# P v with [v|ones] as one full-width stationary operand, q and k loaded in 8-token runs, and layer 1 of the first chunk issued ahead of batch 1's attention

## The chip, the cores and the metric

The kernel runs on one core of one Trainium2 chip. The metric is the device time of one execution in microseconds (us), as the median of several runs. Each run carries a state, fast or slow (a slower state that some executions fall into whatever the kernel); unless a slow run is named, all times, ratios and profiles here are of fast runs. A ratio is the mean time of one kernel's fast runs over the mean of the other's fast runs of the same rounds, on the same chip, so it is not quite the ratio of the medians quoted beside it. The runs were made on several chips, so the cost of a step between two kernels is taken from the difference of their ratios, times 362.4 us. Intervals are 95%.

In the profile PE is TensorE (matmuls and transposes), PEld its weight loads, DVE is VectorE, ACT is ScalarE, POOL is GpSimd. PEclk is the TensorE clock that was granted, as a share of full speed. SBUF is the on-chip memory that the engines work on, PSUM the one that matmuls write to.

## The reference

```python
# q, k, v: [8 batches, 8 heads, 576 tokens, 64], fp32; w_in: [512, 2048]; w_out: [2048, 512]
rel = pos[:, None] - pos[None, :]
mask_local   = (rel >= 0) & (rel < 32)                       # heads 0 to 3
mask_strided = (rel >= 0) & (pos[None] % 32 == pos[:, None] % 32)   # heads 4 to 7
scores = where(mask, (q @ k.T) / 8, -1e9)
attn = softmax(scores)                                       # over the keys
x = concat_heads(attn @ v)                                   # [4608 tokens, 512]
h = x @ w_in
g = where(h > 0, h, exp(min(h, 0)) - 1)                      # ELU
out = g @ w_out                                              # [4608, 512], fp32
```

## The kernel before

The 4608 tokens are nine chunks of 512. A step of layer 1 (`l1`) is four dense matmuls into `hps`, an exp on ScalarE and two VectorE operations that make one block of `g`. A step of layer 2 (`l2`) is four dense matmuls into `ops`. The attention of a batch is cut into 12 pieces: four T (transposes of q and k for a pair of heads) and eight S (scores, exp, mask). Each S leaves an O (P v and the division) to be done one piece later. Pieces are laid between the dense steps, so that TensorE stays busy while ScalarE and VectorE do the softmax.

```python
    p_wk = ctx.enter_context(tc.tile_pool(name="work", bufs=3))
    p_s = ...  # PSUM, 1 buffer of two banks: scores
    p_a = ...  # PSUM, 3 buffers: tp (transposes), o_ps, s_ps
    p_h = ...  # PSUM, 2 buffers: hps
    p_o = ...  # PSUM, 1 buffer: ops
    # [...]
    def piece_T(P):
        for nm, dst in (("q", P.qT[:, 0:S]), ("k", P.kT[:, PRE:PRE + S])):
            ps = p_a.tile([128, S], BF16, tag="a", name="tp")
            # [...] 8 transposes (6 for k of the local heads) into ps
            nc.vector.tensor_copy(dst, ps)
    # [...]
    def piece_O(P, u, pm):
        o_ps = p_a.tile([128, W], F32, tag="a", name="o_ps")
        s_ps = p_a.tile([128, W], F32, tag="a", name="s_ps")
        # local heads:
        for x in range(2):
            nc.tensor.matmul(s_ps[x * D:(x + 1) * D, :], lhsT=ones, rhs=pm[:, x], ...)
        for i in range(3):
            for x in range(2):
                nc.tensor.matmul(
                    o_ps[x * D:(x + 1) * D, i * LQ:(i + 1) * LQ],
                    lhsT=batch_in[P.b]["vl"][:, (P.g0 + x) * LB + 3 * u + i, :],
                    rhs=pm[:, x, i * LQ:(i + 1) * LQ], ...)
        # [...] strided heads: the same with eight matmuls of 72 columns
        nc.scalar.activation(ln, s_ps, ACT.Ln)
        nc.scalar.activation(rc, ln, ACT.Exp, scale=-1.0)      # 1 / sum
        # [...]
        nc.vector.tensor_mul(dst, o_ps..., rc...)              # into xT
    # [...]
    def run_piece(p, lag=0, split=False):
        kind, P, u = p
        flush(lag)                                # O of the older pieces
        if kind == "T":
            piece_T(P)
        else:
            pend.append((P, u, piece_S(P, u, split)))
    # [...] batch 0 alone, then:
    for nb in range(NCH):
        for m in range(MC):
            if nb > 0:
                l2(nb - 1, m)
            if done < len(pieces):
                run_piece(pieces[done], lag=1 if nb == 0 else 0)
                done += 1
            else:
                flush()
            l1(nb, m)
            # [...] load the next batch
```

`s_ps` is read by Ln alone, and only `o_ps` waits for the multiply at the end of the division.

The softmax here doesn't subtract the row's maximum and nothing guards it: scores larger than these inputs give would overflow.

## Time and profile before

| | before |
|---|---|
| time, median of 3 runs | 362.39 us (361.56 to 363.46) |
| TensorE busy | 329.1 us, 91% of the span |
| VectorE, ScalarE busy | 243.8 us, 194.3 us |
| share of TensorE in the chain that ended last | 73% |
| granted clock in the profiled stages from 80 us on | 1.00 |

The first lines are from the page of the kernel before: busy time, the timeline in 40 slices (a digit is the busy share in tenths), and the shares of the engines in the chain of waits that ended last.

```profile
PE 329.1 (91%) x2656; PEld 161.5 (45%) x2656; DVE 243.8 (68%) x501; ACT 194.3 (54%) x377; POOL 92.3 (26%) x120
...
PE   1851986999999999999999999999999999999995
...
PEclk9999999899999999999999999999999999999999
...
PE 73%; DMA 12%; ACT 6%; POOL 4%; issue 2%; DVE 2%; ACTq 0%
```

TensorE is saturated from the eighth slice on (63 us), at full clock from the ninth (72 us), and the chain is mostly its own work. The stage table of the kernel before, for one stretch (columns: stretch, its length, busy time and instructions by engine, granted clock, DMA share, GB/s):

```profile
100.00:125.00 25.00, 24.87 (x237) 12.32 (x235) 20.16 (x42) 16.74 (x34) 8.81 (x11) 1.00 0.81 93
```

TensorE works 24.87 of 25 us. The timeline of the kernel before around one O piece (start, duration, engine, line, operation, output from inputs, count, idle time before and what ended it):

```profile
132.88 0.31 PE L270 MATMUL s_ps<-pm,ones 72*64 72x288 bf16 x2
...
133.03 0.30 PE L279 MATMUL o_ps<-pm,vs 72*64 72x72 bf16 x8
...
133.24 0.41 ACT L297 ACTIVATE ln<-s_ps 128x288 f32<-128x288 f32 x1 [0.52 <-PE s_ps L270]
...
133.26 0.43 PE L211 MATMUL tp<-identity,ql 72*128 72x72 bf16 x8
...
133.68 0.44 ACT L299 ACTIVATE rc<-ln 128x288 f32<-128x288 f32 x1
133.70 0.42 PE L211 MATMUL tp<-identity,kl 96*128 96x96 bf16 x6
...
134.16 0.46 DVE L304 TENSOR_TENSOR xT<-o_ps,rc 128x288 bf16<-128x288 f32 x1 [0.25 <-ACT rc L299]
```

The O piece ends at 133.3 us. The q transposes follow at once, and the k transposes at 133.70, as soon as Ln (133.24 to 133.65) has freed the buffer of `s_ps`. The multiply, at 134.16, holds up nobody.

### The profile page before, as it was taken

The numbers are of one execution on the slowest core, as the hardware profiler recorded it, in microseconds if no ns is written. First come the engines' busy times: TensorE is split into PE (matmuls) and PEld (weight loads), VectorE is DVE, ScalarE is ACT, GpSimd is POOL, SyncE is SP. The second block draws the span as 40 slices with busy tenths as digits, with TensorE's granted clock in tenths as the row PEclk, the third lists the DMA queues.
The fourth block names the chain that finished last, engine by engine and source line by source line (L and its number), as shares of the span: only waits on it lengthen the run. The fifth ranks groups of instructions, "written<-read, shape, count | busy, mean of one in ns | idle before, by whom it ended". The sixth has DMA issues, their size and how long they took to land.

```text
span 361.1 us, 6843 instructions
## 1 busy us (share of the span) xinstructions
PE 329.1 (91%) x2656; PEld 161.5 (45%) x2656; DVE 243.8 (68%) x501; ACT 194.3 (54%) x377; POOL 92.3 (26%) x120
## 2 busy tenths in 40 slices
PE   1851986999999999999999999999999999999995
PEld 1630443454544544445454454444444444444442
DVE  2640797787877877777878777776666666666610
ACT  1650575667566666666666666664444433543411
POOL 7952843958507214510620000000000000000000
PEclk9999999899999999999999999999999999999999
DMA  6999999999959965992960111010111110021122
GB/s 91 113 178 178 107 199 158 99 159 152 142 93 102 96 101 72 87 114 63 119 48 29 31 31 31 29 32 29 46 44 30 34 55 29 29 59 31 30 71 76
DMA packets 88321, 29.03 MB, mean 80 GB/s; under 512 B 72672, under 2 KB 83680, under 8 KB 88288
## 3 DMA queue, kind: packets, MB, share of 16 engines
q0 software_dynamic: 82432, 19.14, 61.7%
q1 hardware_dynamic: 5856, 9.44, 9.1%
q8 instruction: 21, 0.34, 0.4%
q14 instruction: 12, 0.10, 0.1%
HBM read 38.21 MB, written 9.44 MB: 132 GB/s over the span
## 4 chain that ended last, share of the span: by engine, by line
PE 73%; DMA 12%; ACT 6%; POOL 4%; issue 2%; DVE 2%; ACTq 0%
PE ops L382 32%; PE hps L347 30%; DMA vs<-in_v_dram 5%; DMA ks<-in_k_dram 5%; PE tp L211 3%; PE tp L203 2%; PE sc L243 2%; ACT e L251 2%; ACT osb L387 2%; DMA vl<-in_v_dram 2%; DVE pm L259 2%; PE s_ps L286 1%; ACT ln L297 1%; PE s_ps L270 1%; POOL kl L85 1%
## 5 line engine op out<-in xcount | busy, mean ns | idle before, releaser
L347 PE MATMUL hps<-xT,w_in_sb 128*128 128x512 bf16 x576 | 151.4, 386 | 0.2
L382 PE MATMUL ops<-w_out_sb,g 128*128 128x512 bf16 x576 | 145.4, 379 | 0.0
L352 ACT ACTIVATE he<-hps 128x512 f32<-128x512 f32 x144 | 85.8, 596 | 103.7 <-PE hps L347 103.0
L382 PEld LDWEIGHTS <-g 128*128 128x128 bf16 x576 | 56.4, 98 | 68.0
L347 PEld LDWEIGHTS <-w_in_sb 128*128 128x128 bf16 x576 | 50.8, 99 | 53.3 <-issue 2.1
L251 ACT ACTIVATE e<-sc 72x576 bf16<-72x576 f32 (+1 forms) x60 | 38.3, 639 | 17.4 <-PE sc L243 17.4
L297 ACT ACTIVATE ln<-s_ps 128x288 f32<-128x288 f32 x64 | 26.3, 411 | 16.9 <-PE s_ps L270 8.7
L387 ACT COPY osb<-ops 128x512 f32<-128x512 f32 x36 | 21.1, 586 | 20.0 <-PE ops L382 20.0
L76 POOL DMA_DIRECT2D ql<-in_q_dram x32 | 27.2, 855 | 18.0 <-PE tp L211 6.6
L299 ACT ACTIVATE rc<-ln 128x288 f32<-128x288 f32 x64 | 28.4, 443 | 2.0
L85 POOL DMA_DIRECT2D kl<-in_k_dram x32 | 23.7, 758 | 19.7 <-DMA ks<-in_k_dram 5.5
L203 PE MATMUL tp<-identity,qs 72*128 72x72 bf16 x128 | 7.9, 213 | 18.4 <-DMA qs<-in_q_dram 18.4
L304 DVE TENSOR_TENSOR xT<-o_ps,rc 128x288 bf16<-128x288 f32 x32 | 14.6, 456 | 8.3 <-ACT rc L299 7.9
L309 DVE TENSOR_TENSOR xT<-o_ps,rc 128x288 bf16<-128x288 f32 x32 | 14.6, 457 | 7.8 <-ACT rc L299 5.0
L253 DVE TENSOR_TENSOR pm<-e,mask_s 72x576 bf16<-72x576 bf16 x32 | 14.5, 452 | 3.8 <-ACT e L251 2.4
L259 DVE TENSOR_TENSOR pm<-e,mask_l 128x576 bf16<-128x576 bf16 x32 | 14.6, 457 | 2.5 <-ACT e L251 0.5
L203 PEld LDWEIGHTS <-qs 72*128 72x128 bf16 x128 | 5.8, 108 | 19.9 <-DMA qs<-in_q_dram 18.7
L67 POOL DMA_DIRECT2D vs<-in_v_dram x8 | 5.7, 710 | 31.9 <-PE sc L243 31.6
L96 POOL DMA_DIRECT2D vl<-in_v_dram x8 | 9.6, 1197 | 11.8 <-PE tp L203 11.4
L286 PE MATMUL s_ps<-pm,ones 128*64 128x288 bf16 x64 | 10.6, 322 | 1.6 <-DVE pm L259 0.9
L203 PE MATMUL tp<-identity,ks 72*128 72x72 bf16 x128 | 7.9, 214 | 3.9 <-DMA ks<-in_k_dram 3.6
L291 PE MATMUL o_ps<-pm,vl 128*64 128x96 bf16 x192 | 10.6, 215 | 0.7 <-DMA vl<-in_v_dram 0.7
(343 smaller groups left out, 338.5 us busy)
## 6 DMA issues: line engine op xcount, KB each, us to landing
out_dram<-osb SPq DMA_DIRECT2D x32, 144.0 KB
qs<-in_q_dram POOLq DMA_DIRECT2D x8, 288.0 KB, 5.9
ks<-in_k_dram POOLq DMA_DIRECT2D x8, 288.0 KB, 7.7
vs<-in_v_dram POOLq DMA_DIRECT2D x8, 288.0 KB, 7.9
ql<-in_q_dram POOLq DMA_DIRECT2D x32, 72.0 KB, 6.3
kl<-in_k_dram POOLq DMA_DIRECT2D x32, 72.0 KB, 4.2
vl<-in_v_dram POOLq DMA_DIRECT2D x8, 288.0 KB, 5.5
w_in_sb<-in_moe_w_in_dram POOLq DMA_DIRECT2D x4, 512.0 KB, 10.9
```

The lines of the kernel that those rows point to most:

```text
L76: nc.gpsimd.dma_start(out=t[:, h // 2, :, h % 2, :], in_=q[b, h].rearrange("(p s) d -> p s d", s=NS))
L85: nc.gpsimd.dma_start(out=t[:, h // 2, :, h % 2, :], in_=src[b, h].rearrange("(t p) d -> p t d", p=LQ))
L203: nc.tensor.transpose(ps[:, o:o + RS], src[:, P.g0 + x, 2 * sp * D:2 * (sp + 1) * D], identity[0:RS, 0:RS])
L251: nc.scalar.activation(e[0:R], sc[0:R, :, 0:W], ACT.Exp, scale=scale)
L259: nc.vector.tensor_mul(pm, e, mb.unsqueeze(1).to_broadcast([128, 2, W]))
L297: nc.scalar.activation(ln, s_ps, ACT.Ln)
L299: nc.scalar.activation(rc, ln, ACT.Exp, scale=-1.0)
L304: nc.vector.tensor_mul(dst, o_ps.rearrange(pat, z=2, sp=2), rc.rearrange(pat, z=2, sp=2))
L347: nc.tensor.matmul(hps, lhsT=w_in_sb[:, cc, m * 128:(m + 1) * 128], rhs=xT[:, cc, nb * CHUNK:(nb + 1) * CHUNK], start=(c == 0), stop=(c == ...
L352: nc.scalar.activation(e, hps, ACT.Exp)
L382: nc.tensor.matmul(ops, lhsT=g[:, m, kk * 128:(kk + 1) * 128], rhs=w_out_sb[:, m, :], start=(m == 0), stop=(m == MC - 1))
L387: nc.scalar.copy(o_sb, ops)
```

## The change

The intent has three parts.

- **P v (P).** The separate ones matmuls go. The stationary operand (the one that is loaded as weights, PEld, before the other streams through) becomes [v|ones] for the first head of a pair and [ones|v] for the second, 128 columns wide, so that one matmul gives both P v and the sums. The two heads then need one PSUM tile each. Two Ln of 64 partitions and two multiplies of 64 partitions replace one each of 128, and both PSUM tiles live until the multiply. For the strided heads VectorE first spreads the loaded v into that layout (`vs`).
- **Loads (L).** q and k of the local heads come in runs of 8 tokens, as one transfer each instead of four. The local heads must be paired on the chip (GpSimd copies `qlp`, `klp`), and the k transposes come out in another order of tokens, which the copy out of PSUM undoes.
- **Order (S).** All of layer 1 of chunk 0 is issued before batch 1's attention, which then runs without dense steps beside it. Later pieces are spread over a chunk's 16 steps, 1.2 steps apart.

```diff
+    def spread_v(b):                       # two VectorE copies per batch
+        t = vss[b % 2]
+        src = batch_in[b]["vr"].rearrange("p (g x) (s d) -> p x g s d", x=2, d=D)
+        for x in range(2):
+            nc.vector.tensor_copy(t[:, :, :, 2 * x * D:(2 * x + 1) * D], src[:, x])
+    def pair_up(b, nm):                    # four GpSimd copies per batch from batch 2 on
+        [...]
+            nc.gpsimd.tensor_copy(t[:, :, :, x, :], src[:, x])
 [... loads ...]
 # piece_T, local heads
+                if nm == "k":
+                    dst = dst.rearrange("c (p s) -> c s p", s=NS)
+                    ps = ps.rearrange("c (s p) -> c s p", s=NS)
             nc.vector.tensor_copy(dst, ps)
 [...]
 # piece_O
-        o_ps = p_a.tile([128, W], F32, tag="a", name="o_ps")
-        s_ps = p_a.tile([128, W], F32, tag="a", name="s_ps")
+        o_ps = [p_a.tile([128, W], F32, tag="a", name=f"o_ps{x}") for x in range(2)]
 [... the ones matmuls go; local heads, strided alike: ]
+            for x in range(2):
+                for i in range(3):
                     nc.tensor.matmul(
-                        o_ps[x * D:(x + 1) * D, i * LQ:(i + 1) * LQ],
-                        lhsT=batch_in[P.b]["vl"][:, (P.g0 + x) * LB + 3 * u + i, :],
+                        o_ps[x][:, i * LQ:(i + 1) * LQ],
+                        lhsT=vt[:, P.g0 // 2, 3 * u + i, x * D:(x + 2) * D],
-        nc.scalar.activation(ln, s_ps, ACT.Ln)
+        nc.scalar.activation(ln[lo], o_ps[0][hi], ACT.Ln)
+        nc.scalar.activation(ln[hi], o_ps[1][lo], ACT.Ln)
         nc.scalar.activation(rc, ln, ACT.Exp, scale=-1.0)
-            nc.vector.tensor_mul(dst, o_ps..., rc...)
+        for x, pr in ((0, lo), (1, hi)):
+            [...] nc.vector.tensor_mul(xs[pr, ...], o_ps[x][pr], rc[pr])
 [... main loop ...]
+    for m in range(MC):
+        l1(0, m)
+    for i in range(PB, 2 * PB):
+        run_piece(pieces[i], lag=1, split=(pieces[i][0] == "S" and pieces[i][2] == 1))
+    flush()
+    for nb in range(1, NCH):
+        [... sorted list of l2 steps, pieces and l1 steps ...]
+            at = [8 + 0.7 * i if nb == 1 else 0.1 + 1.2 * i for i in range(PB)]
```

## The prediction

> **What bounds it now.** From about 62 us on TensorE is the limit: in the table by stages it is busy 24.87 of 25 us at 100 to 125 us. Dense 512-column matmuls follow each other every 0.216 us (timeline: four in 0.86 us), so 1152 of them are 249 us. Until 62 us the timeline shows loads and latency: TensorE waits 9.4 us for batch 1's q, then VectorE and ScalarE set the pace while chunk 0's first layer is mixed with batch 1's attention. Later a step (4+4 dense) takes 1.73 us alone, about 2.49 us with an attention piece: a batch of 12 pieces costs TensorE about 9.1 us.
>
> **Removed.** The ones matmuls: s_ps plus o_ps take 0.37 us per piece; eight (or six) full-width ones should take 0.24. That is about 1 us a batch, 6 to 7 us in all. The small runs of q and k go; v should land about 2.6 us earlier (20.3 before) and w_in by 28 us. The 8.7 us of idle before batch 1 goes.
>
> **Added, with measured durations.** A second Ln per piece (0.41 us ScalarE), a second xT multiply (0.457 us VectorE), two VectorE copies of v a batch (estimate 0.4 to 0.7 us each), strided k copies, four GpSimd copies a batch. VectorE per chunk with attention: 16 x 1.12 + about 16 = 34 us, against 29.
>
> **Moved, and this decides.** Three PSUM buffers serve o_ps and tp. Before, the k transpose after an O piece took the buffer of s_ps and waited only for Ln (o_ps at 133.03 us, k transposes at 133.70, right after Ln). In the built order of after, both halves stay until Ln, Ln, Exp and multiply are done, and the k transpose waits for the multiply of the O piece just ahead: 0.41+0.41+0.44+0.46 plus handovers, about 2.1 us after that piece starts, of which 0.5 us is filled. Estimated stall: 1.4 to 1.6 us at the second and third transposes of each batch, 0.7 us at the fourth; before 0.2 each. The first O piece also waits for the v copies, behind a layer-1 pair on VectorE: about 1.8 us. Sum about 5 us a batch on the saturated engine, against 1 us saved and 0.9 us of old waits.
>
> **Path.** Startup: batch 0 ends about 28.5 us (25.1 before; ScalarE 1.95 instead of 1.5 us a piece), layer 1 of chunk 0 is VectorE-bound at 1.13 us x 16, to 47, batch 1 alone to about 65. Before had the same work done by the equivalent of 65.5: no gain. Chunk 1 packs 12 pieces into eight steps, latency-bound: 42 to 47 us against 37. Chunks 2 to 6: about 38.5 each against 36.7. The last 73 us are unchanged.
>
> **Prediction: 374 us, 8 in 10 within 355 to 390.** Faster by over 2%: 0.17; within 2%: 0.25; slower by over 2%: 0.58.
>
> **What would show it.** No s_ps group; waits of the k transposes for the xT multiply and of O for the vs copy, 1 to 2 us each, as gaps in TensorE after 66 us; chunk 0's layer 1 at about 29 to 47 us; second layer from about 70 us.
>
> **What would make it wrong.** Startup ending well before 60 us, stalls hidden because fewer pieces meet a buffer in use, or, the other way, GpSimd's copies slowing VectorE. The Trainium skill ("TensorEngine Tiling (Array Packing)", Key Properties) says changing the tiling mode drains TensorE; the trace's 0.95 us from four dense matmuls to s_ps, against 0.86, agrees. If such drains are most of the 9.1 us, the gain is larger.

## The result, and the profile after

| | before | after |
|---|---|---|
| time, median | 362.39 us | 450.62 us (449.77 to 451.29) |
| ratio | | 1.244 [1.238, 1.251] |
| TensorE busy | 329.1 us (91%) | 345.1 us (77%) |
| VectorE, ScalarE busy | 243.8, 194.3 us | 316.5, 222.7 us |

The change made the kernel 24% slower. The direction was predicted; 374 us (355 to 390) was far too small. The same lines of the page of after:

```profile
PE 345.1 (77%) x2582; PEld 168.3 (37%) x2624; DVE 316.5 (70%) x572; ACT 222.7 (50%) x445; POOL 102.3 (23%) x130
...
PE   2557745597677787878777877788779779999995
...
PEclk9999975596889989989999999998998999999998
...
PE 46%; DVE 29%; ACT 18%; issue 4%; DMA 1%; POOL 0%; ACTq 0%
PE hps L363 19%; PE ops L398 19%; DVE kT L238 7%; DVE g L372 5%; ACT rc L317 5%; ACT ln L315 4%; DVE xT L325 4%; ACT ln L314 4%; DVE xT L321 4%; DVE he L370 3%; ACT he L368 3%; DVE pm L282 2%; PE o_ps L307 2%; PE o_ps L298 2%; PE tp L217 2%
```

TensorE is no longer saturated: 104 us of its span are idle, against 32 before (span less busy time). In the chain its share fell from 73% to 46%. VectorE and ScalarE now hold 47%, with `kT`, `ln`, `rc`, `xT` and `g` by name. TensorE's busy time rose by 16 us, although the change takes matmul work away; its mean clock was lower (0.93 to 0.95 in its runs, 0.99 to 1.00 in the fast ones of the kernel before). So of the 88 us between the two profiles 72 are more idle time of TensorE and 16 are longer busy time. The stage table of after around the lone attention of batch 1:

```profile
50.00:60.00 10.00, 5.74 (x36) 2.47 (x35) 8.09 (x16) 3.58 (x6) 3.63 (x6) 1.00 1.52 171
60.00:70.00 10.00, 4.48 (x83) 3.48 (x85) 6.87 (x13) 4.39 (x10) 7.45 (x9) 0.54 0.68 80
70.00:80.00 10.00, 4.95 (x91) 3.64 (x89) 9.07 (x12) 5.82 (x14) 0.75 (x1) 0.50 0.60 86
80.00:90.00 10.00, 6.77 (x39) 3.14 (x39) 5.91 (x13) 6.12 (x14) 4.20 (x5) 0.50 0.59 38
100.00:125.00 25.00, 18.37 (x159) 8.64 (x161) 16.36 (x30) 11.08 (x24) 0.00 (x0) 0.80 0.07 22
```

The clock falls to a half at about 60 us and is still at a half from 80 to 90 us. TensorE is busy 18.37 of 25 us in the stretch where before it was busy 24.87. The timeline of after, at the first O piece of a batch:

```profile
149.39 0.64 PE L298 MATMUL o_ps<-pm,vs 72*128 72x72 bf16 x8 [1.34 <-DVE vs L85]
...
149.73 0.41 ACT L314 ACTIVATE ln<-o_ps 64x288 f32<-64x288 f32 x1 [1.91 <-PE o_ps L298]
...
149.87 0.42 PE L217 MATMUL tp<-identity,qs 72*128 72x72 bf16 x8
...
150.16 0.40 ACT L315 ACTIVATE ln<-o_ps 64x288 f32<-64x288 f32 x1
150.60 0.44 ACT L317 ACTIVATE rc<-ln 128x288 f32<-128x288 f32 x1
151.07 0.94 DVE L321 TENSOR_TENSOR xT<-o_ps,rc 64x288 bf16<-64x288 f32 x2 [1.40 <-ACT rc L317]
151.57 0.42 PE L217 MATMUL tp<-identity,ks 72*128 72x72 bf16 x8 [1.28 <-DVE xT L321]
```

This is the wait that was predicted. The q transposes (149.87) take the third buffer. The k transposes need one of the two that the O piece holds, and so wait for Ln, Ln, Exp and the first multiply, until 151.57: 1.28 us of idle TensorE. The O piece itself had waited 1.34 us for the spread of v. A second kind of wait was not predicted; it shows in the timeline of after somewhat later:

```profile
168.27 0.41 ACT L314 ACTIVATE ln<-o_ps 64x288 f32<-64x288 f32 x1 [0.40 <-PE o_ps L298]
...
168.30 0.30 PE L266 MATMUL sc<-qT,kT 64*128 64x96 bf16 x6
...
168.70 0.40 ACT L315 ACTIVATE ln<-o_ps 64x288 f32<-64x288 f32 x1
169.14 0.44 ACT L317 ACTIVATE rc<-ln 128x288 f32<-128x288 f32 x1
...
169.49 0.63 ACT L274 ACTIVATE e<-sc 128x576 bf16<-128x576 f32 x1
169.61 0.94 DVE L321 TENSOR_TENSOR xT<-o_ps,rc 64x288 bf16<-64x288 f32 x2 [0.56 <-ACT rc L317]
...
170.59 0.46 DVE L282 TENSOR_TENSOR pm<-e,mask_l 128x576 bf16<-128x576 bf16 x1
...
171.10 0.42 PE L307 MATMUL o_ps<-pm,vl 128*128 128x96 bf16 x6 [0.67 <-DVE pm L282]
```

The scores of the next piece are done at 168.6. Their exp starts at 169.49 only, as it stands behind Ln, Ln and Exp of the older piece in ScalarE's order. Then the mask multiply (`pm`, 170.59) stands behind the two multiplies of the older piece on VectorE (169.61 to 170.55). The next O piece starts 0.67 us late. All of TensorE's waits in after, by releaser (total, number, longest):

```profile
PE o_ps L307 <- DVE pm L282: 19.2, 26, 2.0
PE o_ps L298 <- DVE vs L85: 12.7, 8, 3.5
PE sc L266 <- DVE kT L238: 10.8, 7, 2.1
PE tp L226 <- DVE xT L321: 8.9, 6, 1.5
PE tp L217 <- DVE xT L321: 7.7, 6, 1.3
```

Added up by what TensorE waited for, over all lines of this table: `xT` (the multiply) 30.6 us, `pm` 25.3, `vs` 12.7, `kT` 10.8, `g` 6.4. In the kernel before, the same table has, loads aside, 0.6 us for `kT`, 1.5 us for `pm` and 1.9 us for Ln; its two longest such lines are:

```profile
PE tp L211 <- ACT ln L297: 1.5, 2, 0.7
PE s_ps L286 <- DVE pm L259: 0.9, 2, 0.7
```

The groups of after that stand behind these waits:

```profile
L238 DVE COPY kT<-tp 128x576 bf16<-128x576 bf16 x32 | 50.6, 1581 | 1.8 <-PE tp L217 1.8
...
L321 DVE TENSOR_TENSOR xT<-o_ps,rc 64x288 bf16<-64x288 f32 x64 | 29.1, 455 | 24.2 <-ACT rc L317 23.2
...
L314 ACT ACTIVATE ln<-o_ps 64x288 f32<-64x288 f32 x64 | 26.1, 407 | 46.1 <-PE o_ps L298 24.3 <-PE o_ps L307 21.2
```

The first Ln and the first multiply are shown; the second of each is there 64 times as well, at 0.402 and 0.455 us. An Ln over 64 partitions takes 0.40 us, like one over 128 (0.411 before), and the half multiply takes 0.455 us like the whole one (0.457 before). Halving the partitions saves nothing: the cost doubles. The copy to `kT` takes 1.58 us in the mean, because the 16 copies of local heads take 2.69 to 2.74 us each.

### The profile page after: what moved, and what is told of

Same layout as the page of the kernel before. It is cut to its first block, busy times and chain, and to the rows that moved or that the text cites. A ratio compares the mean times of both kernels' runs of the same rounds, so it can differ in the third digit from the quotient of the medians.

```text
span 449.1 us, 6886 instructions
## 1 busy us (share of the span) xinstructions
PE 345.1 (77%) x2582; PEld 168.3 (37%) x2624; DVE 316.5 (70%) x572; ACT 222.7 (50%) x445; POOL 102.3 (23%) x130
## 4 chain that ended last, share of the span: by engine, by line
PE 46%; DVE 29%; ACT 18%; issue 4%; DMA 1%; POOL 0%; ACTq 0%
PE hps L363 19%; PE ops L398 19%; DVE kT L238 7%; DVE g L372 5%; ACT rc L317 5%; ACT ln L315 4%; DVE xT L325 4%; ACT ln L314 4%; DVE xT L321 4%; DVE he L370 3%; ACT he L368 3%; DVE pm L282 2%; PE o_ps L307 2%; PE o_ps L298 2%; PE tp L217 2%
## 5 line engine op out<-in xcount | busy, mean ns | idle before, releaser
L372 DVE TENSOR_TENSOR g<-he,hps 128x512 bf16<-128x512 bf16 x144 | 99.0, 688 | 5.1
L370 DVE TENSOR_SCALAR he<-he 128x512 bf16<-128x512 f32 x144 | 63.4, 440 | 53.3 <-ACT he L368 52.6
L238 DVE COPY kT<-tp 128x576 bf16<-128x576 bf16 x32 | 50.6, 1581 | 1.8 <-PE tp L217 1.8
L93 POOL COPY qlp<-ql 72x1024 bf16<-72x1024 bf16 x12 | 13.2, 1127 | 157.6 <-PE tp L226 157.6
L314 ACT ACTIVATE ln<-o_ps 64x288 f32<-64x288 f32 x64 | 26.1, 407 | 46.1 <-PE o_ps L298 24.3
L321 DVE TENSOR_TENSOR xT<-o_ps,rc 64x288 bf16<-64x288 f32 x64 | 29.1, 455 | 24.2 <-ACT rc L317 23.2
L325 DVE TENSOR_TENSOR xT<-o_ps,rc 64x288 bf16<-64x288 f32 x64 | 29.1, 455 | 23.8 <-ACT rc L317 19.7
L107 POOL DMA_DIRECT2D vl<-in_v_dram x32 | 28.4, 893 | 32.2 <-PE o_ps L307 7.3
L298 PE MATMUL o_ps<-pm,vs 72*128 72x72 bf16 x256 | 17.3, 211 | 20.9 <-DVE vs L85 12.7
L307 PE MATMUL o_ps<-pm,vl 128*128 128x96 bf16 x192 | 16.1, 221 | 22.0 <-DVE pm L282 19.2
L315 ACT ACTIVATE ln<-o_ps 64x288 f32<-64x288 f32 x64 | 25.7, 402 | 2.6 <-PE o_ps L307 1.1
L266 PE MATMUL sc<-qT,kT 64*128 64x72 bf16 (+1 forms) x392 | 18.4, 213 | 10.8 <-DVE kT L238 10.8
## 6 DMA issues: line engine op xcount, KB each, us to landing
vr<-in_v_dram POOLq DMA_DIRECT2D x8, 288.0 KB, 10.8
```

Source lines behind the costliest of these rows:

```text
L298: nc.tensor.matmul(o_ps[x][:, i * RS:(i + 1) * RS], lhsT=vt[:, P.g0 // 2, 4 * u + i, x * D:(x + 2) * D], rhs=pv[:, x, z, sp * RS:(sp + 1) ...
L314: nc.scalar.activation(ln[lo], o_ps[0][hi], ACT.Ln)
L315: nc.scalar.activation(ln[hi], o_ps[1][lo], ACT.Ln)
L321: nc.vector.tensor_mul(xs[pr, u * W:(u + 1) * W], o_ps[x][pr], rc[pr])
L325: nc.vector.tensor_mul(dst, o_ps[x][pr].rearrange(pat, b=3, s=NS), rc[pr].rearrange(pat, b=3, s=NS))
L370: nc.vector.tensor_scalar(e1, e, scalar1=1.0, scalar2=1.0, op0=ALU.min, op1=ALU.subtract)
```

## The experiments

Three theories were on the table after the result. **A**: the slow k copies of 2.7 us are the main cause. **B**: the new P v is, by its second Ln, its second multiply and the two PSUM tiles that it holds. **C**: the new order is. Every kernel below gives a correct result unless it says otherwise.

### Undoing one part: a1, a2, a3, and the copy alone, a4

**a1_kswap**: after, but the k copy writes contiguously and reads PSUM with a step.

```diff
-                    dst = dst.rearrange("c (p s) -> c s p", s=NS)
+                    dst = dst.rearrange("c (p s) -> c p s", s=NS)
-                    ps = ps.rearrange("c (s p) -> c s p", s=NS)
+                    ps = ps.rearrange("c (s p) -> c p s", s=NS)
```

> After with one change: the local k copy writes its bf16 elements in address order and reads PSUM strided instead (same values). Theory A, the 16-byte-strided bf16 write costs the 2.7 us and sits on the critical chain (kT is 7% of the chain, 31 us): the copies fall to 0.45 to 0.8 us, VectorE loses about 32 us of busy time and the kernel comes to 405 to 422 us. Rival B, the buffer waits of the prediction are the real limit and the long copies run beside them: 438 to 452 us. Rival C, any strided access costs as much, the PSUM read too: copies stay over 2 us, time unchanged.

Measured: 437.59 us, the median of three fast runs, ratio 1.211 [1.206, 1.216]. A fourth run, the profiled one, was slow (447.8 us); with it the median is the 438 us that later texts quote. The gain is 12 us of the 88. A falls as the main cause.

**a2_oldpv**: after with the old `piece_O` (ones matmul, one Ln, one multiply), reading v from the new layout.

```diff
-        o_ps = [p_a.tile(...) for x in range(2)]
+        o_ps = p_a.tile([128, W], F32, tag="a", name="o_ps")
+        s_ps = p_a.tile([128, W], F32, tag="a", name="s_ps")
 [... the rest of piece_O as before the change]
```

> After with the old P v alone: 64-wide v and a separate ones matmul, one Ln, one multiply, same loads and order. Theory B (k transposes wait for Ln, Ln, Exp, multiply): their waits for the xT multiply vanish, 410 to 425 us. Rival A (the strided k copy decides): the stalls move to the copy, 435 to 450 us.

Measured: 405.78 us, ratio 1.124 [1.118, 1.129]. Half of the loss comes back with one part undone, more than had been expected. B is the largest part, even while the slow k copies stay.

**a3_oldsched**: after with the old main loop.

```diff
-    for m in range(MC):
-        l1(0, m)
-    for i in range(PB, 2 * PB): [...]
+    [the loop of the kernel before, with pair_up added]
```

> After with the issue order of before (layer 1 of chunk 0 mixed with the attention of batch 1, one piece per step from then on), loads and P v of after. If the order alone costs what the startup shows (first layer of chunk 1 starts at 87 us, the equivalent before is 65.5): 420 to 432 us. If loads and P v set the startup too and the order is neutral: 440 to 455 us. If the slower issue of pieces hides stalls worse: over 455.

Measured: 455.19 us, ratio 1.260 [1.253, 1.267]. With the new P v and the slow copies in place, the old order is a little worse than the new one. C is not the main cause.

**a4_bench**: the kernel before with a row of copies at its end, each twice, 128 partitions by 576 elements.

```diff
+        nc.vector.tensor_copy(xo, xps)                                           # PSUM to SBUF
+        nc.vector.tensor_copy(xo...("c (p s) -> c s p", s=8), xps...("c (s p) -> c s p", s=8))   # writes 16 bytes apart
+        nc.vector.tensor_copy(xo...("c (p s) -> c p s", s=8), xps...("c (s p) -> c p s", s=8))   # reads apart, writes dense
+        [... steps of 4 and 8 bytes, SBUF source, fp32, ScalarE, GpSimd]
```

> Before plus copies of 128x576 at its end, two of each, alone: PSUM bf16 to SBUF bf16 contiguous (0.45 us expected), with 16-byte destination stride (2.6 to 2.7 us if the cost is the instruction's own; about 0.76 us[...], if the 2.7 us came from other engines' traffic), with strided PSUM read and contiguous write (0.76 us), with strides of 4 and 8 bytes, SBUF to SBUF contiguous and strided, fp32 destination strided, and the strided write on ScalarE and GpSimd (if the cost is in SBUF's partial writes, all engines slow down; if it is VectorE's own, ScalarE stays near 0.65 us).

Measured, one look with a profile (390.97 us with the copies in it). The groups of a4, in order of cost; L423 is the dense copy, L424 writes 16 bytes apart, L425 reads PSUM apart and writes densely, L429 is L424 with an SBUF source:

```profile
L424 DVE COPY xo<-xps 128x576 bf16<-128x576 bf16 x2 | 5.4, 2700 | 0.1
...
L429 DVE COPY xo<-xsb 128x576 bf16<-128x576 bf16 x2 | 2.9, 1442 | 0.1
...
L425 DVE COPY xo<-xps 128x576 bf16<-128x576 bf16 x2 | 1.5, 758 | 0.1
...
L423 DVE COPY xo<-xps 128x576 bf16<-128x576 bf16 x2 | 0.9, 458 | 18.7 <-PE xps L421 11.7 <-POOL xo L434 7.0
```

The 2.7 us are the instruction's own and do not come from contention: 2.70 us alone. Writes 4 and 8 bytes apart took 0.80 and 1.43 us. Swapping the two sides of the copy, as a1 does, brings it to 0.76 us. ScalarE and GpSimd slow down alike with writes 16 bytes apart (0.64 to 2.70 us, and 0.66 to 2.73 us from SBUF), so the cost is not a peculiarity of VectorE; why the copy on VectorE from SBUF takes only 1.44 us is open. So theory A had found a real cost, one that is worth 12 us beside the others.

### Combining: b1, b2, b3, b4

**b1_kswap_oldpv**: the edits of a1 and a2 together; **b2_kswap_tfirst**: a1 with the transposes issued ahead of the O piece; **b3_pv_only**: the new P v with its v loads alone, old q and k loads, old order; **b4_loads_only**: the new loads with the dense k copy, old P v reading v as loaded, old order.

```diff
 # b2, in the main loop
-                run_piece(pieces[(nb + 1) * PB + i])
+                piece = pieces[(nb + 1) * PB + i]
+                if piece[0] == "T":
+                    piece_T(piece[1])
+                    flush()
+                else:
+                    run_piece(piece)
 # b4, in the old piece_O
-                            lhsT=batch_in[P.b]["vs"][:, P.g0 + x, s * D:(s + 1) * D],
+                            lhsT=batch_in[P.b]["vr"][:, P.g0 + x, s * D:(s + 1) * D],
```

> After with the k copy written in address order and the old P v: order and loads of after stay. If the two costs are separate they add: 450 - 12 - 45 = 393 us. If, with the buffer waits gone, the k copy became the critical piece (its share of the chain rose from 7 to 11%, 44 us), more comes back: 370 to 385 us. What is left over 362 is then the order of issue with VectorE's pace in the startup.

Measured: 381.17 us, ratio 1.049 [1.045, 1.053]. From a1 to b1 only P v changes, and 59 us come back. From a2 to b1 only the k copy changes, and 27 us come back, twice what a1 had shown. The two causes overlap: while P v holds everything up, the faster copies help less.

> After with the address-order k copy (438 us) and one move: from chunk 1 on a transpose piece is issued ahead of the P v piece that stood before it, not behind it; work and buffers are the same. Theory B1, the new P v costs through the k transposes' wait for the multiply of the piece just ahead (about 1.4 us, 18 times, plus the lower clock): 405 to 420 us. Theory B2, it costs through the added work of ScalarE and VectorE or through the buffers that two halves hold, wherever the wait stands: 430 to 445 us.

Measured: 413.83 us, ratio 1.142 [1.136, 1.149]. With the transposes ahead, TensorE's long waits for the multiply at the transposes go, and 25 us against a1 come back. The wait for a held buffer is therefore a cause and not just a sign. The rest stays.

> The new P v alone, with its v loads: q and k loaded as before, the order of before. If P v alone brings the waits (prediction: 5 us a batch less 2 us, over seven batches, so 20 us): 378 to 395 us. If it only hurts together with the order of after: 358 to 368 us. If every piece in the old order meets a buffer in use, since O and T stand side by side there too: 395 to 420 us.

Measured: 442.0 us, the mean of two fast runs (441.6, 442.4); ratio 1.218 [1.215, 1.221]. The new P v alone, in an otherwise old kernel, costs 79 us (0.218 of 362.4). This was beyond every branch. In its profile TensorE waits 46.7 us for the multiply and 19.7 for `pm`.

> The new loads alone: q, k in 8-token runs with the k copy in address order, GpSimd pairing, v from the run tile; P v and order of before. If the startup was short of DMA as its waits say (9.4 us for batch 1's q): 350 to 358 us. If the unpaired transposes and GpSimd's copies take it back: 360 to 370 us.

Measured: 360.15 us, ratio 0.992 [0.989, 0.994]. The loads, with a dense k copy, are a small gain.

### Inside P v: c1, c2, c3, d1

The first two and the last of these give a wrong result.

**c1_oneln**: a1 with one activation over the 128 partitions of the first tile in place of the two Ln. **c2_oneln_onemul**: c1 with one multiply over 128 partitions of the first tile, so that the second tile has no reader. **d1_oneln_firsthalf**: c1 with both multiplies, but both read the first tile, so that the second has no reader.

```diff
 # c1
-        nc.scalar.activation(ln[lo], o_ps[0][hi], ACT.Ln)
-        nc.scalar.activation(ln[hi], o_ps[1][lo], ACT.Ln)
+        nc.scalar.activation(ln, o_ps[0], ACT.Exp, scale=-1.0)
 # c2, besides
-        for x, pr in ((0, lo), (1, hi)):
+        for x, pr in ((0, slice(0, 2 * D)),):
 # d1: c1, and
-                nc.vector.tensor_mul(xs[pr, u * W:(u + 1) * W], o_ps[x][pr], rc[pr])
+                nc.vector.tensor_mul(xs[pr, u * W:(u + 1) * W], o_ps[0][pr], rc[pr])
```

> Wrong result on purpose. The address-order copy kernel (438 us) with one activation over all 128 partitions of the first half in place of two Ln of 64 (an Exp, so that no negative number meets Ln): ScalarE loses 0.4 us a piece and both halves are freed 0.4 us earlier. If ScalarE's extra pass is the main cost of the new P v (it delays the next exp and so pm): 400 to 415 us. If the hold of both halves until the multiply is: 420 to 430 us. Neither: 435 to 440.

Measured: 411.11 us, ratio 1.134 [1.127, 1.140]. The second activation costs 28 us against a1, although ScalarE is busy only half of the span. How it costs that is not parted here: c1 also frees both tiles 0.4 us earlier. TensorE's waits for the multiply (`xT`) fall from 32.7 us in a1, whose profiled run is slow, to 17.5, and those for `pm` from 16.7 to 10.9, so more of the gain shows in the hold of the tiles than in the later exp.

> Wrong result on purpose. As the one before, and one multiply of 128 partitions in place of two of 64; the second half has no reader, so its buffer is free at once. TensorE does the new P v, ScalarE and VectorE the old amount. It should come to the old-P-v kernel (381 us) less what full-width matmuls save TensorE, 6 to 8 us if 0.13 us a piece is right: 368 to 378 us. Over 390 would say that something else in the new P v costs (the v copies, the full-width matmuls themselves).

Measured: 372.78 us, ratio 1.031 [1.026, 1.035]. Another 37 us. It is also 8 us below b1, from which it differs in the wide matmuls and in what reads them: the saving that the change was made for is real (6.7 us by the difference of the ratios, within about 2). In the profiles TensorE is busy 13.5 us less than in b1 (325.0 against 338.5, at a clock of 0.972 against 0.961) and idle 3.7 us more.

> Wrong result on purpose: c1_oneln (411.1 us), but both multiplies read the first PSUM half, so the second has no reader and comes free as soon as its matmuls are done; VectorE does the same two multiplies as in c1. Taking one multiply away as well gave 372.8. Theory H (the 38 us are the hold of two of the three PSUM buffers until the multiply): 373 to 382, most of the 38 us come back. Theory V (they are VectorE's time for the second multiply, which delays everything behind it): 402 to 411. Between them: both. I expect 385 to 398, both, because a freed second half removes the wait of the k transposes but VectorE remains 0.45 us longer per piece.

Measured: 385.19 us, ratio 1.065 [1.060, 1.070]. The hold of the second tile costs 25 us (c1 to d1), and the second multiply 12 (d1 to c2). In d1 both multiplies read the first tile, which so is held one multiply longer than in c2; the 12 us contain that too. TensorE's waits between 80 and 300 us in c1:

```profile
PE o_ps L298 <- DVE vs L85: 7.7, 6, 1.3
PE tp L226 <- DVE xT L320: 5.3, 5, 1.1
PE o_ps L307 <- DVE pm L282: 5.0, 14, 1.5
```

and in d1:

```profile
PE o_ps L298 <- DVE vs L85: 7.7, 6, 1.3
PE o_ps L307 <- DVE pm L282: 5.0, 16, 1.6
```

The waits of the transposes for the multiply (`tp <- xT`) are gone from d1, while those for `vs` have the same 7.7 us. Over the whole span the waits for `xT` are 17.5 us in c1, 4.7 in d1 and none in c2.

**c3_pieces_first**: b2 with the score pieces, too, issued ahead of the older O.

```diff
-                    run_piece(piece)
+                    pend.append((piece[1], piece[2], piece_S(piece[1], piece[2])))
+                    flush(1)
```

> The transposes-first kernel (414 us) with the score pieces too ahead of the older P v piece, so that ScalarE gets the next exp before the two Ln and the Exp of that piece. If O waits for pm because exp stands behind them (1.0 to 1.3 us each in the trace): 395 to 405 us. If the wait is elsewhere: 410 to 418 us.

Measured: 409.96 us, ratio 1.133 [1.129, 1.137]. A miss: only 4 us below b2. The waits for `pm` fall from 14.2 us (local heads, b2) to 3.4. Those for `xT` rise from 15.3 to 18.7 us and those for the `qT` copies from 5.8 to 7.9, and TensorE is busy 6.7 us longer (340.3 against 333.6) at a lower clock (0.948 against 0.964). So part of the wait moved elsewhere, and part of the gain went with the clock; why the clock was lower was not tested.

### The order and the loads: c4, d2, e1, e2, d3, d4

**c4_loads_order**: b4 with each piece ahead of the layer-2 step and the older O behind it.

```diff
-            if nb > 0:
-                l2(nb - 1, m)
             if done < len(pieces):
-                run_piece(pieces[done], lag=1 if nb == 0 else 0)
+                [nb > 0:] piece_T(P) or pend.append((P, u, piece_S(P, u)))
+                l2(nb - 1, m)
+                flush(1 if kind == "S" else 0)
```

> Loads alone (360.2 us) with another order from chunk 1 on: the piece, four second-layer matmuls, the older P v, four first-layer matmuls, so that no transpose stands directly behind a P v piece. If the 0.2 us waits of the k transposes before (four a batch, six batches: 5 us) are real and nothing new waits: 353 to 357 us. If they only move: 359 to 362 us.

Measured: 373.68 us, ratio 1.033 [1.027, 1.038]. A miss, 14 us worse than b4. The new waits are those of `o_ps` for Ln, 22 of them with 10.8 us together: the O piece now asks for a buffer that the Ln of the O piece before it has not yet let go. Why it is not free by then was not tested.

**d2_order_only**: old loads of q and k, old P v, new order.

```diff
-            items += [(at[0] + 0.3 * i, 3, nm) for i, nm in enumerate(("ql", "kl"))]
+            [load_run(q, ...) and load_run(k, ...) of the local heads are the old loads again]
```

> The new order alone: old q and k loads, old P v. From the pairs of runs so far (b1 381.2 with order and loads, b4 360.2 with loads alone) the order costs about 21 us. Theory O (the order itself costs, because batch 1's attention runs alone and chunk 1 packs 12 pieces into eight steps): 378 to 386. Theory G (the order is harmful only together with the GpSimd copies of the new loads): 360 to 370.

Measured: 366.17 us, ratio 1.013 [1.007, 1.018]. The order, with the new loads of v that stay in this kernel, costs about 4.5 us. Before this run b1 less b4, 21 us, had looked like the price of the order; that reading fell.

**e1_order_loads**: b1 with the old P v reading v as loaded, so that the VectorE copies `vs` go. **e2_order_loads_nopair**: e1 without the GpSimd copies of q and k.

```diff
 # e1
-        if "vs" not in batch_in[P.b]:
-            spread_v(P.b)
 # e2, besides
-            items += [(at[0] + 0.3 * i, 3, nm) for i, nm in enumerate(("ql", "kl"))]
```

> b1_kswap_oldpv (381.2 us) with old P v reading the loaded v directly, so that the two VectorE copies of v per batch are gone too: what remains of the change is the order and the loads with a contiguous k copy. In b1 the first O piece of a batch waited 1.1 us for those copies, 8.3 us in all. If that is all of what b1 has over order and loads: 372 to 375, and the order costs some 13 us beside the new loads but only 4.5 us alone (d2 366.2). If order and loads simply add (366.2 x 0.992): 361 to 366. If the copies did not matter: 379 to 382.

Measured: 368.27 us, the median of three fast runs, ratio 1.014 [1.008, 1.020]. The result lies between two branches. Two VectorE copies of 0.44 us per batch (mean in b1) cost 12.7 us in all, more than the 8.2 us for which TensorE visibly waits on them in b1. Where the rest of it arises is open, as e1 has no profile of a fast run.

> e1 without any of the GpSimd copies of q and k: 16 half-height transposes for each local q and k tile instead of 8. If GpSimd's copies are why order and loads are worse together than their sum: 363 to 368. If they are not: equal to e1, or up to 5 us above it, for 32 more transposes a batch at 0.05 us each are 1.6 us of TensorE a batch.

Measured: 366.61 us, ratio 1.010 [1.004, 1.015]. In the same rounds on the same chip the four runs of e2 (366.46 to 366.89) all lie below the three fast ones of e1 (368.16 to 368.51). So without the copies the kernel is 1.7 us faster, although it has the extra transposes; what the copies cost by themselves is not parted from what these add.

**d3_lead4**: b4 with the first four layer-1 steps of chunk 0 ahead of batch 1's first piece, in the old loop. **d4_lead4_pair3**: d3 without the GpSimd copies for batch 2.

```diff
 # d3
-            if done < len(pieces):
+            if done < len(pieces) and (nb > 0 or m >= 4):
 # d4, besides
-                if done % PB == 0 and done >= 2 * PB:
+                if done % PB == 0 and done >= 3 * PB:
```

> b4_loads_only (360.2 us) with the first four layer-1 steps of chunk 0 ahead of batch 1's first piece, so that TensorE has dense work in its wait of 4.7 and 1.9 us for batch 1's q and k. If the wait is what costs: 354 to 358. If batch 1's attention, delayed by four steps, is the critical chain at the start (VectorE- and ScalarE-bound until 62 us): 360 to 366.

Measured: 354.61 us, ratio 0.980 [0.976, 0.984], five rounds. This version is faster than both kernels, than before by 1.6 to 2.4%. TensorE's waits up to 75 us in b4:

```profile
PE tp L220 <- DMA qs<-in_q_dram: 11.2, 2, 6.5
```

and in d3:

```profile
PE tp L220 <- DMA qs<-in_q_dram: 6.5, 1, 6.5
```

Batch 0's wait at the very start (6.5 us) remains, and the 4.7 us for batch 1's q are filled with dense steps. The intent of the new order was right, and four steps are enough for it. With all sixteen (d2, which differs from d3 in the loads and in the later order too) batch 1's attention has no dense work left beside it: the mean clock in d2 from 60 to 80 us is 0.76, in d3 1.00.

> d3 with the GpSimd copies of q and k left out for batch 2, whose q and k transposes are then 16 half-height ones each as in batch 0. In b4 VectorE's ELU operation took up to 2.5 us more while those copies ran at 57.6 to 60.6 us. If they share a memory port with it: 1 to 3 us below d3. If not: equal to d3 or 1 us above (twice the transposes).

Measured: 356.18 us, ratio 0.985 [0.981, 0.989]. It is not below d3, but this does not clear the copies: the stall only moved to the next batch. In d3 the mask multiply took 4.24 us beside the copies of batch 2 (`qlp` from 58.31, `klp` to 62.29):

```profile
58.37 4.24 DVE L279 TENSOR_TENSOR pm<-e,mask_s 72x576 bf16<-72x576 bf16 x1
```

In d4 it takes its usual 0.45 us for that batch, but the copies of batch 3 (70.58 to 74.56) meet an ELU operation that otherwise takes 0.43 us:

```profile
70.23 4.62 DVE L380 TENSOR_SCALAR he<-he 128x512 bf16<-128x512 f32 x1
```

TensorE then waits for `pm` 3.18 us in d3 (until 62.66) and 3.49 us in d4 (until 75.98), so each run has one such wait. In b4 the same ELU operation took 4.59 us (57.28), which is more than the expectation says.

### The sum

Read as a ladder, each kernel differs from the one above it in what the second column names. The last column is the difference of the ratios times 362.4 us; with the intervals of the two ratios a step is uncertain by 2 to 3 us, so that of e1 is not clear of zero. The steps depend on their order, as a2 and b1 showed for the k copy.

| kernel | added against the line above | ratio | us |
|---|---|---|---|
| before | | 1.000 | |
| d2 | new order, new loads of v | 1.013 | +4.5 |
| e1 | new loads of q and k, GpSimd copies, dense k copy | 1.014 | +0.6 |
| b1 | spread of v on VectorE | 1.049 | +12.7 |
| c2 | full-width P v, one reader of one tile | 1.031 | -6.7 |
| d1 | second multiply, first tile held for it | 1.065 | +12.4 |
| c1 | second tile held until the multiply | 1.134 | +24.9 |
| a1 | second Ln, both tiles held 0.4 us longer | 1.211 | +28.2 |
| after | k copy with writes 16 bytes apart | 1.244 | +12.0 |

c2, d1 and c1 give wrong results: their lines tell the time of the work named and nothing else.

## Why the prediction was right or wrong

**Right: what bounds the kernel.** TensorE was saturated from 62 us on, and 72 of the 88 us are added idle time of TensorE.

**Right: what is saved on TensorE.** "6 to 7 us in all" was predicted, and c2 against b1 shows 6.7, within about 2; that it agrees to a tenth is luck. The Trainium skill ("TensorEngine Tiling (Array Packing)", Key Properties) says that changing the tiling mode drains TensorE, and the prediction allowed for a larger gain from fewer such changes. The trace agrees: four dense matmuls take 0.86 us before the full-width P v in c2, and 0.96 us before the 64-wide `s_ps` in b1. But where score matmuls follow, the P v group of c2 takes 0.34 to 0.36 us to their start, against 0.26 before transposes, so some of the gap only moved. An estimate for 64 pieces is up to 7 us from the shorter matmuls (0.37 us a piece in b1 and 0.26 in c2, before transposes) and up to 6 from the gap; which of them makes up the 6.7 us stays open, as no run isolates a drain.

**Right: the mechanism and the size of one wait.** 1.4 to 1.6 us were predicted for the k transposes behind an O piece, and 1.28 and up to 1.5 us measured. These waits of the transposes and those for `vs` were put at about 5 us a batch, so 35 us for seven batches; the table of waits has 25.0 us for `xT` at transposes and 12.7 for `vs`, 37.7 together. Another 5.6 us of waits for `xT` stand at other matmuls.

**Wrong: the sum.** "Sum about 5 us a batch on the saturated engine, against 1 us saved and 0.9 us of old waits" is the step that failed, and with it "Chunks 2 to 6: about 38.5 each against 36.7" (46.6 each were measured) and "layer 1 of chunk 0 is VectorE-bound at 1.13 us x 16, to 47, batch 1 alone to about 65". The path did not even carry its own sum: 5 less 1 less 0.9 is 3.1 us a batch, and it added 1.8. The predicted and measured terms, with boundaries read from TensorE's timeline and from the last output copy of each chunk:

| stretch | predicted | measured |
|---|---|---|
| start to the end of batch 1's attention | 65 us | 85.4 us |
| chunk 1 | 42 to 47 (43.5 in the sum) | 56.0 (85.4 to 141.4) |
| chunks 2 to 6 | 5 x 38.5 = 192.5 | 233.1 (141.4 to 374.5) |
| the rest | 73 | 74.6 (374.5 to 449.1) |

Three things were left out of the sum, and the runs show each.

1. *The O pieces' waits for `pm`*, 25.3 us. For these chunks the prediction counted the second Ln only in the hold of the buffers. It also stands ahead of the next exp on ScalarE, and the second multiply ahead of the next mask multiply on VectorE, as the timeline at 168 to 171 us shows. Taking one activation away (a1 to c1) gave back 28.2 us, part of it through the shorter hold. The new P v is not alone in this: `pm` waits are 19.7 us in b3 (new P v, dense copies), 25.7 in a2 (old P v, slow k copies, which stand ahead of the mask multiply on VectorE) and 5.9 in b1, which has neither.
2. *The k copies*. The prediction named "strided k copies" and gave them no duration, as nothing in the trace of before had that pattern. They take 2.7 us, not the 0.46 us of the dense copy. They cost 12 us in the full change, and 27 us without the other delays (a2 to b1).
3. *The startup and the clock.* Layer 1 of chunk 0 ran at about 1.45 us a step from 35 to 59 us: with nothing between its steps, each waits for one of two PSUM buffers to pass through exp and two VectorE operations, and the bound is that latency, not VectorE's 1.13 us of work. Then batch 1 ran alone to 85.4 us, with TensorE idle half of the time, and the granted clock fell to 0.50. The order is not what makes this long: in d2, with the same order, the same pace of layer 1 and a clock of 0.50 as well (58 to 66 us), but the old P v and dense copies, batch 1's attention ends at 65.0 us, just where the prediction had put it. The Trainium skill ("TensorE: Matmul & The Clock Gate", Part 1: The HAM clock gate) says that a clock gate sets TensorE's clock by how busy it has recently been, at half or full rate. The trace agrees: 0.54, 0.50 and 0.50 in the three stretches from 60 us, with TensorE busy for 45 to 68% of the time. How much of the 88 us is the clock and how much the waits alone was not separated; the 16 us of longer busy time are the part that shows as such. A clock that falls because of waits is counted with them in the ladder.

**Too narrow: the hold was taken for the whole cost.** On the ladder the hold of the second tile until the multiply is 24.9 us; the second Ln is 28.2, and the second multiply and the spread of v are 25.1 together. The second Ln and the second multiply lengthen the hold as well as the queues, and no run parts the two, so the share of the hold is at least the 24.9 us. For chunks 2 to 6 the prediction saw only what a tile's life does to the next user of its buffer and what the spread of v delays, and not what longer queues on the two other engines do to every later piece.

**A danger that was real but small: GpSimd's copies.** "GpSimd's copies slowing VectorE" was listed as a danger. The Trainium skill ("GPSIMD Engine Reference", 1. Specifications) says that GpSimd's SBUF interfaces are shared with VectorE, with contention for VectorE instructions that have two SBUF inputs or run in a two-port performance mode. The traces agree with contention, though they do not show the mode: in after a mask multiply at 61.48 us, which usually takes 0.45 us, took 2.56 us while the GpSimd copies ran (59.75 to 63.7 us). On the whole time it is little: one wait of TensorE of 3.2 to 3.5 us in d3 and d4, and 1.7 us between e1 and e2.

## What to carry to other kernels

Merging two matmuls into one wider one can save a saturated TensorE a little and still lose much, if what reads the result doubles: here 64 partitions cost ScalarE and VectorE as much as 128 (0.40 and 0.46 us). Cost such a change by the chain from the matmul to the next use of its PSUM buffer, and also by what each added instruction delays behind it on its engine; an engine that is half idle on average can still set the pace (c1: 28 us from one activation a piece). To fill a wait for a load, move only as much dense work ahead as covers it (four steps here, 2% faster): all sixteen steps left batch 1's attention with nothing beside it, at a clock of 0.50.

## What the Trainium skill lacked or had wrong

- "SBUF — State Buffer" (Door 1: The DMA port swizzle) says that accesses within one 16-byte line run at full bandwidth, so that a bf16 operand can step by up to 8 elements for free. The copies measured by themselves in a4 differ from 8 bytes on: PSUM to SBUF on VectorE, 128 x 576 bf16, took 0.46 us dense, 0.76 with reads apart and dense writes, 0.80 with writes 4 bytes apart, 1.43 at 8 bytes and 2.70 at 16 bytes.
- "Vector Engine (DVE) Microarchitecture Reference" (5.2 Measured stream behaviour on trn2) gives 2.50 to 2.51 ns per column for a destination that steps by 24 words. The copy from SBUF with writes 16 bytes apart comes to the same figure with a smaller step and bf16: 1.44 us for 576 elements is 2.50 ns each, the start of the instruction included. The section has no figure for a bf16 destination with a PSUM source, which took 2.70 us or 4.7 ns an element (1.41 us with an fp32 destination, 32 bytes apart). ScalarE took 2.70 us for the same copy.
- "TensorE: Matmul & The Clock Gate" (Part 1: The HAM clock gate) and the summary table of that page tell to avoid idle gaps of more than about 3 us, but not what share of busy time keeps or regains the clock. In after, TensorE busy 5.74 of 10 us kept 1.00 (50 to 60 us). The mean of 0.54 from 60 to 70 us puts the fall at about 60.8 us, just behind an idle stretch of 2.08 us, and 4.95 and 6.77 busy us of 10 did not regain the clock in the next 20 us.
